# Top-k attention and two feed-forward stages on one core: the masks move to ScalarE, and the late weight matrices land elsewhere

## The chip, the cores and the metric

One core of a Trainium2 chip runs the whole program in one launch. The metric is device time in microseconds. The kernel before takes 1127.8 us, the median of three runs (1126.94 to 1128.36).

## The reference

Attention over 4 batches, 8 heads, 576 tokens of width 64, in which each query keeps its 32 largest scores; then two feed-forward blocks on 2304 tokens of width 512.

```python
scores = (q @ k.transpose(0, 1, 3, 2)) / sqrt(64)
kth = np.partition(scores, -32, axis=-1)[..., -32:-31]     # 32nd largest of each row
scores = np.where(scores >= kth, scores, -1e9)
scores = scores - scores.max(axis=-1, keepdims=True)
attn = np.exp(scores); attn = attn / (attn.sum(-1, keepdims=True) + 1e-9)
x = (attn @ v).transpose(0, 2, 1, 3).reshape(2304, 512)
h = x @ w_in                       # 512 -> 2048
x = np.maximum(0.01 * h, h) @ w_out            # 2048 -> 512
h = np.maximum(np.maximum(x @ w1, x @ w2), x @ w3)   # 512 -> 768, three times
y = h @ w_out2                     # 768 -> 512
```

The inputs are float64; the kernel takes their bit patterns as pairs of 32-bit words.

## The kernel before

**Precision.** Each float32 operand of a product is split into two float16 parts (high, and the rest, low), and three matmuls stand for one (`three`, L871). So most tiles get a ScalarE pass that writes the high part and a GpSimd subtraction that writes the low part.

**Attention.** There are 72 steps, each of two row tiles j = 0, 1 of 128 queries against 576 keys: 64 full steps (one head pair, 128 queries) and 8 steps for the last 64 queries of a batch. A step: queries times keys on PE into PSUM (L715); ScalarE copies the scores into S (L720); VectorE finds the 32nd largest value of a row in seven passes per tile, MAX8 (L735) and MATCH_REPLACE8 (L737) in turn, in the tile w; GpSimd works out a bias from the largest value (L775, L780); ScalarE writes pp = exp(scale * S + bias) with scale and bias as per-partition columns (L785). Then the mask: for j = 0 VectorE does (S >= threshold) * pp in one operation (L790); for j = 1 it writes S >= threshold as float16 over S (L794) and GpSimd multiplies pp by that (L797). ScalarE copies pp to float16 (L799), GpSimd subtracts for the low part (L801), a DMA transposes phl into pt (L804), and PE multiplies with the values (L830 to L832). There are three S, one w, one pp, one phl and one pt. Four steps finish 128 tokens of all heads (two steps for the last 64); transposes (L866) then bring them into xu, the input of a feed-forward unit.

**Feed-forward.** The 2304 tokens are ten units of 192, 128, seven times 256, and 192 tokens. A unit has a first half (`h_tile`, `y_acc`: w_in, the leaky maximum as a Prelu at L920, w_out) and a second half (`m_tile`, `o_acc`: three products, their maximum on VectorE at L1017, the last product). Unit 0's second half and all of unit 1 wait for all weights.

**Weights.** `prep_w` (L467) loads float64 words (L482), joins the words to float32 in three dependent VectorE operations per chunk of up to 512 columns (L496, L499, L502) through a PSUM tile, finds a scale, and splits into float16 parts that stay on the core. w_in has 8 parts of 1024 columns, w_out 8 of 1024, w123 18 of 512, the last matrix 8 of 384. Memory is full, so landing tiles and float32 tiles lie in zones of the weight tiles that are filled later (`ZONE`, L270). Markers such as `ZA`, `ZB`, `ZR` order the users of a zone: the landing tiles of w123 (`rw`) lie in the last matrix's region and wait for `ZB`, and the last matrix lands in the two xu buffers:

```python
"rw": [w2f[:, 2048 * i:2048 * i + 2048].bitcast(F32) for i in range(3)],   # in ZONE
...
ZT = "xu"                                                                # landing tag of the last matrix
```

**Order.** Nothing runs by itself in the order of the code. `Plan` (L72 on) collects all operations with an assumed duration, dependencies and a priority `pr`, plays them through a list schedule in which each engine takes the earliest ready operation, and of those ready within `eps` (0.03 us) the one of lowest `pr`; buffers are handed out from the counts in `NB` (L230). The resulting order is emitted, and each engine runs its part of it strictly in order. A dependent operation of the same engine is assumed to be ready 0.1 to 0.15 us after its predecessor (`LAT`). Weight operations have lower `pr` than all but the first attention steps. For w123 and the last matrix one PSUM tile (`hW`: 1) is allowed to conversion at a time.

Of the kernel before, what the change touches and what calls it, by code (L numbers as in the profile page):

```python
# [20 lines left out]
S2 = S // 2  # L21
# [185 lines left out]
def dve(n, fast=False):  # L207
    return (n / (2 if fast else 1) / 0.96 + 69) / 1000
# [11 lines left out]
def attention_moe_kernel(ctx, tc, qk, v, w_in, w_out, w123, w2o, outT):  # L220
# [31 lines left out]
    def fbuf(tag, ph, shape, dt=F32):  # L252
# [21 lines left out]
            "rw": [w2f[:, 2048 * i:2048 * i + 2048].bitcast(F32) for i in range(3)],  # L274
# [84 lines left out]
    def prep_qk(b, hp, pr, fast):  # L359
        d = dr.tile([2, 2, 2, D, S], F16, name=f"dqk{b}_{hp}")  # L360
        use_ring(("qk", b % 2, hp), 11)
        bi = col(2)
        kb = ("es", b, hp)
        for a in (1, 0):
# [19 lines left out]
        es, es2 = col(), col(2)  # L384
        op(POOL, 0.32, lambda: G.tensor_tensor(es, bi[:, 0:1], bi[:, 1:2], op=ALU.mult),
           r=[(("qk", b, hp, a), "b") for a in range(2)], w=[(kb, 0)], pr=pr)
        op(POOL, 0.32, lambda: G.tensor_scalar(es2[:, 0:1], es, 0.125, None, op0=ALU.mult),
           r=[(kb, 0)], w=[(kb, 1)], pr=pr)
        op(POOL, 0.32, lambda: G.tensor_scalar(es2[:, 1:2], es, -0.125, None, op0=ALU.mult),
           r=[(kb, 0)], w=[(kb, 2)], pr=pr)  # L390
# [69 lines left out]
    ZT = "xu"  # L460
    CVK = "iotz"
    CW = 512
    CVX = 0.0
# [3 lines left out]
    def prep_w(kind, c, parts, hi, lo, colnorm, n2c, s, bi, pr, tags, guard=((), (), []), gate=()):  # L467

        key = ("w", kind, c)
        zr = {"ra": ["ZR"], "rw": ["ZB"]}.get(tags[0], [])  # L470
        zf = {"fi": ["ZA"], "ft": ["ZA", "ZR", ("ZF", c)], "fz": ["ZB", ("ZZ", c)]}.get(tags[1], [])
        if guard[0]:
            op(POOL, 0.0, lambda: None, w=guard[0], pr=pr)
        fs, sq = [], []
        plan.eps = WEPS
        for i, saps in enumerate(parts):
            nf = sum(n for _, n in saps)
            f = buf(tags[1], [P, 768 if tags[1] in ("raw", "xu") else 512], I32)
            o = 0
            for sap, n in saps:  # L480
                raw = buf(tags[0], [P, 768])
                op(SP, 0.55, lambda raw=raw, sap=sap, n=n: Y.dma_start(raw().bitcast(I64)[:, :n], sap),  # L482
                   w=([(f, "ld")] if tags[1] in ("raw", "xu", "k2") or tags[0] in ("raw", "xu") else []) + [raw, (key, "ld")],
                   r=list(gate) + zr + (zf + [("l1", hp, a) for hp in range(HP) for a in range(2)] * (kind == "z" and ZT == "raw") + guard[2] * (tags[1] in ("raw", "xu")) if kind in "tz" else []), pr=PRW0 if (kind, c) == ("i", 0) else pr,
                   dma=dma(P * n * 8))
                for q in range(0, n, CW):
                    cw = min(CW, n - q)
                    w = lambda raw=raw, q=q, cw=cw: raw().bitcast(I32)[:, 2 * q:2 * (q + cw)].rearrange("p (n t) -> p n t", t=2)
                    t = lambda f=f, cw=cw, q=q + o: f()[:, q:q + cw]
                    pb = None  # L490
                    if kind in CVK:
                        pb = buf("acc", [P, 2, UN]) if kind in "io" else fbuf("h", "W", [P, 512])
                    m = t if pb is None else (lambda pb=pb, cw=cw, two=kind in "io": (
                        pb().rearrange("p a n -> p (a n)") if two else pb()).bitcast(I32)[:, :cw])
                    mk_ = [(f, o)] if pb is None else [pb]
                    op(DVE, dve(cw, pb is None) + CVX * (pb is not None), lambda w=w, m=m: V.tensor_scalar(  # L496
                        m(), w()[:, :, 1], 3, 0x3FFFFFFF, op0=ALU.logical_shift_left, op1=ALU.bitwise_and),
                       r=[raw] + zr + zf, w=mk_, pr=pr)
                    op(DVE, dve(cw) + CVX * (pb is not None), lambda w=w, m=m: V.scalar_tensor_tensor(  # L499
                        m(), w()[:, :, 0], 29, m(), op0=ALU.logical_shift_right, op1=ALU.bitwise_or),  # L500
                       r=[raw] + zr + zf, w=mk_, pr=pr)
                    op(DVE, dve(cw) + CVX * (pb is not None), lambda w=w, t=t, m=m: V.scalar_tensor_tensor(  # L502
                        t(), w()[:, :, 1], -0x40000000, m(), op0=ALU.bitwise_and, op1=ALU.bitwise_or),
                       r=[raw] + zr + zf + mk_ * (pb is not None), w=[(f, o)], pr=pr)
# [74 lines left out]
    def w1_prep(f, pr):  # L579
# [4 lines left out]
               (["ZA", "ZB"] if f == 0 else [], ["ZR"] if f == 0 else [("ZF", f - 2)] if f >= 3 else [],  # L584
                ["ZR"] if f < 3 else [("ZF", f - 2)]), gate=GATES[2])

    def w2_prep(e, pr):
        for hp in range(HP) if ZT == "raw" else ():
            if (1, hp) not in seen:
                seen.add((1, hp))  # L590
                prep_batch(1, hp)
        prep_w("z", e, [[(w2o[e, i], 384) for i in range(2)]], [w2[:, e, 0]], [w2[:, e, 1]],
               None, c1(cz, e), c1(sz, e), c1(bz, e), pr, (ZT, "fz" if e < 3 else ZT),
               ({0: ["ZB"], 3: [("ZZ", 2)]}.get(e, []), [("ZZ", e - 1)] if e in (1, 2) else [],
                [("ZZ", e - 1)] if e else ["ZB"]))
# [80 lines left out]
    EXPP = 4  # L676
# [3 lines left out]
    FM = 1  # L680

    def fused(i, j):
        return j < FM

    NBE = POOL
    NG, ND = (G, 0.34) if NBE == POOL else (V, 0.1)
    MODE = "N"
    NF0 = 0

    def fold(i):  # L690
        return "N" if i < NF0 else MODE

    def attention(i):
# [8 lines left out]
        Sp, wp, m = buf("S", [P, 2, S]), buf("w", [P, 2, 2, S2]), buf("m", [P, 2, TOPK + TOPK // 2 + 1])  # L702
# [19 lines left out]
        md = fold(i)  # L722
        KM = TOPK // 2
        if md == "N":
            thr = lambda j: m()[:, j, TOPK - 1:TOPK]
            tk = lambda j: [(m, j, 0, 3)]
            wj = lambda j: wp()[:, j].rearrange("p x s -> p (x s)")
            for g in range(7):
                for j in range(2):
                    r = g // 2  # L730
                    mc = lambda j=j, r=r: m()[:, j, 8 * r:8 * r + 8]
                    src = (lambda j=j: Sb[j]()) if g < 2 else (lambda j=j: wj(j))
                    rd = [(Sp, j)] if g < 2 else [(wp, j, 0)]
                    if g % 2 == 0:
                        op(DVE, dve(S) * 1.03, lambda mc=mc, src=src: V.max(mc(), src()), r=rd, w=[(m, j, 0, r)], pr=pd)  # L735
                    else:
                        op(DVE, dve(S) * 1.03 + 0.06, lambda mc=mc, src=src, j=j: V.match_replace(  # L737
                            out=wj(j), in_to_replace=mc(), in_values=src(), imm_value=NEG),
                           r=[(m, j, 0, r)] + rd, w=[(wp, j, 0)], pr=pd)
        else:  # L740
            thr = lambda j: m()[:, j, TOPK + KM:]
            tk = lambda j: [(m, j, 2)]
            for x, o in ((0, ALU.max), (1, ALU.min)):
                E, eng, du = (G, POOL, 1.32) if md == "P" else (V, DVE, 0.83)
                op(eng, du, lambda x=x, o=o, E=E: E.tensor_tensor(wp()[:, :, x], Sp()[:, :, :S2], Sp()[:, :, S2:], op=o),
                   r=[(Sp, 0), (Sp, 1)], w=[(wp, 0, x), (wp, 1, x)], pr=pd)
            for x, g in [(0, 0), (0, 1), (1, 0), (0, 2), (1, 1), (0, 3), (1, 2), (0, 4), (0, 5), (0, 6)]:
                for j in range(2):
                    r, c0 = g // 2, TOPK * x + 8 * (g // 2)
                    mc = lambda j=j, c0=c0: m()[:, j, c0:c0 + 8]  # L750
                    wx = lambda j=j, x=x: wp()[:, j, x]
                    if g % 2 == 0:
                        op(DVE, 0.375, lambda mc=mc, wx=wx: V.max(mc(), wx()), r=[(wp, j, x)], w=[(m, j, x, r)], pr=pd)
                    else:
                        op(DVE, 0.427, lambda mc=mc, wx=wx: V.match_replace(
                            out=wx(), in_to_replace=mc(), in_values=wx(), imm_value=NEG),
                           r=[(m, j, x, r)], w=[(wp, j, x)], pr=pd)
            op(DVE, 0.2, lambda: V.tensor_tensor(m()[:, :, TOPK:TOPK + KM], m()[:, :, TOPK:TOPK + KM],
                                                 m()[:, :, TOPK - 2:TOPK - 2 - KM:-1], op=ALU.min),
               r=[(m, j, 0, r) for j in range(2) for r in range(1, 4)], w=[(m, j, 1, r) for j in range(2) for r in range(2)],  # L760
               pr=pd)
            op(DVE, 0.2, lambda: V.tensor_reduce(m()[:, :, TOPK + KM], m()[:, :, TOPK - 1:TOPK + KM], axis=AX.X,
# [427 lines left out]
```

## Time and profile before

| | |
|---|---|
| median of 3 runs | 1127.8 us |
| profiled execution, first to last instruction | 1133.3 us |
| TensorE (PE) matmul busy | 918.0 us, 81% |
| VectorE (DVE) busy | 968.7 us, 85% |
| ScalarE (ACT) busy | 757.2 us, 67% |
| GpSimd (POOL) busy | 678.2 us, 60% |

The profile shows one execution; what lies around its first and last instruction isn't in it, and its span is 5.5 us above the median of the runs. Busy times are shares of the whole span; the kernel has stages with different limits, so the views by stage matter more. Matmuls overlap in the pipeline: a 256-column matmul lasts 0.27 us in the rows, and the next starts 0.11 us after it.

### The profile page before, as it was taken

What the parts mean: (1) busy time and instruction counts of PE and PEld (TensorE: products, weight loads), DVE (VectorE), ACT (ScalarE), POOL (GpSimd) and SP (SyncE); (2) the same over time, 40 slices, a digit from 0 to 9 for tenths busy, and PEclk for the clock granted to TensorE, in tenths of its full rate; (3) what the DMA queues carried; (4) which work ended last, traced back from release to release, by engine and by line L of the source; (5) the groups of instructions that cost most, each with busy time, mean ns of one, the idle gap of its engine ahead of it and who ended that gap; (6) DMA issues with size and microseconds to landing.
All of it is one profiled execution on the core that took longest, in us unless ns stands there. A gap on an engine that the chain in (4) does not pass through costs nothing.

```text
span 1133.3 us, 27397 instructions
## 1 busy us (share of the span) xinstructions
PE 918.0 (81%) x10292; PEld 803.0 (71%) x10292; DVE 968.7 (85%) x2154; ACT 757.2 (67%) x1625; POOL 678.2 (60%) x1054
## 2 busy tenths in 40 slices
PE   2253246763798998998999999889989999899998
PEld 1142235662698987887878788778878888788998
DVE  3999999899999998999898999889989998994101
ACT  7588749886578666567877766677786666555242
POOL 5476557765558565467777645666875565455221
PEclk9999997785799999999999999999999999999999
DMA  8759356766344434345673334553763443432000
GB/s 297 233 123 269 130 152 198 189 173 118 95 101 87 97 62 78 62 86 133 154 175 81 83 67 91 78 134 73 158 150 68 90 62 60 73 63 53 25 1 16
DMA packets 268517, 125.79 MB, mean 111 GB/s; under 512 B 237408, under 2 KB 255328, under 8 KB 266336
## 3 DMA queue, kind: packets, MB, share of 16 engines
q1 hardware_dynamic: 268384, 124.04, 47.1%
q8 instruction: 81, 1.33, 0.5%
q14 instruction: 52, 0.43, 0.1%
HBM read 62.65 MB, written 14.16 MB: 68 GB/s over the span
## 4 chain that ended last, share of the span: by engine, by line
PE 36%; DMA 13%; ACT 7%; POOL 5%; DVE 4%; issue 4%; SPq 1%; POOLq 0%; ACTq 0%; DVEq 0%
DMA pt<-phl 10%; PE h L872 6%; PE h L873 6%; PE h L874 6%; PE acc L872 4%; PE acc L873 4%; PE acc L874 4%; PE s L715 2%; POOL phl L801 2%; PE h L830 2%; DVE m L735 1%; DMA raw<-in_v 1%; DVE w L737 1%; PE h L831 1%; PE h L832 1%
## 5 line engine op out<-in xcount | busy, mean ns | idle before, releaser
L735 DVE MAX8 m<-w 128x8 f32<-128x576 f32 x432 | 309.1, 747 | 0.0
L933 POOL TENSOR_TENSOR f16t<-k,f16t 128x256 f16<-128x256 f32 (+2 forms) x220 | 143.0, 652 | 195.7 <-ACT f16t L927 167.9
L737 DVE MATCH_REPLACE8 w<-m,w 128x576 f32<-128x576 f32 x288 | 212.1, 742 | 0.0
L801 POOL TENSOR_TENSOR phl<-pp,phl 128x576 f16<-128x576 f32 x144 | 184.0, 1284 | 41.0 <-ACT phl L799 39.4
L872 PE MATMUL h<-k,w 128*128 128x256 f16 (+2 forms) x720 | 190.1, 268 | 8.9 <-ACT k L1013 4.6
L873 PE MATMUL h<-k,w 128*128 128x256 f16 (+2 forms) x720 | 190.1, 268 | 2.7 <-POOL k L975 2.5
L874 PE MATMUL h<-k,w 128*128 128x256 f16 (+2 forms) x720 | 189.9, 267 | 0.0
L873 PE MATMUL acc<-f16t,wo 128*128 128x256 f16 (+2 forms) x640 | 166.6, 264 | 4.4 <-POOL f16t L933 4.4
L872 PE MATMUL acc<-f16t,wo 128*128 128x256 f16 (+2 forms) x640 | 166.7, 264 | 1.2 <-ACT f16t L927 0.6
L874 PE MATMUL acc<-f16t,wo 128*128 128x256 f16 (+2 forms) x640 | 166.6, 264 | 0.0
L872 PE MATMUL h<-xu,wi 128*128 128x256 f16 (+1 forms) x576 | 154.8, 269 | 2.2 <-DVE k L502 1.3
L873 PE MATMUL h<-xu,wi 128*128 128x256 f16 (+1 forms) x576 | 154.7, 269 | 0.0
L874 PE MATMUL h<-xu,wi 128*128 128x256 f16 (+1 forms) x576 | 154.7, 269 | 0.0
L715 PE MATMUL s<-kt,qt 128*128 128x288 f16 (+5 forms) x800 | 109.1, 287 | 55.2 <-ACT S L720 48.4
L799 ACT ACTIVATE phl<-pp 128x576 f16<-128x576 f32 x144 | 97.1, 681 | 78.2 <-DMA pt<-phl 29.1
L785 ACT ACTIVATE pp<-S,nb,colt 128x576 f32<-128x576 f32 x144 | 120.9, 861 | 14.4 <-POOL nb L775 8.0
L830 PE MATMUL h<-vt,pt 128*128 128x65 f16 (+1 forms) x800 | 92.3, 203 | 45.9 <-DMA pt<-phl 37.7
L797 POOL TENSOR_TENSOR pp<-pp,S 128x576 f32<-128x576 f32 x72 | 92.1, 1279 | 56.9 <-DVE S L794 44.1
L927 ACT ACTIVATE f16t<-k 128x256 f16<-128x256 f32 (+2 forms) x220 | 86.2, 392 | 54.5 <-DVE k L1017 51.7
L920 ACT ACTIVATE k<-h,colt 128x256 f32<-128x256 f32 (+2 forms) x160 | 71.7, 452 | 73.1 <-PE h L874 71.4
L830 PEld LDWEIGHTS <-pt 128*128 128x128 f16 (+1 forms) x800 | 81.0, 106 | 54.6 <-DMA pt<-phl 52.5
L715 PEld LDWEIGHTS <-qt 128*128 128x128 f16 (+1 forms) x800 | 64.9, 109 | 75.3 <-issue 59.8
(136 smaller groups left out, 2644.8 us busy)
## 6 DMA issues: line engine op xcount, KB each, us to landing
w<-in_w SPq DMA_DIRECT2D x18, 512.0 KB, 4.4
w<-in_w_in SPq DMA_DIRECT2D x8, 1024.0 KB, 7.0
w<-in_w_out SPq DMA_DIRECT2D x8, 1024.0 KB, 4.9
raw<-in_qk SPq DMA_DIRECT2D x24, 288.0 KB, 3.4
dqk<-hl SPq DMA_DIRECT2D x48, 144.0 KB, 2.6
kt<-dqk SPq DMA_DIRECT2D x16, 288.0 KB, 3.1
qt<-dqk SPq DMA_DIRECT2D x144, 32.0 KB, 2.2
raw<-in_v SPq DMA_DIRECT2D x12, 352.0 KB, 3.7
```

The costliest lines, as they stand in the source:

```text
L715: T.matmul(p()[osl, h, o:o + w], q()[:, hh, st, :n], k()[:, hh, kc:kc + w], start=st == 0, stop=st == 1, skip_group_check=True)
L735: op(DVE, dve(S) * 1.03, lambda mc=mc, src=src: V.max(mc(), src()), r=rd, w=[(m, j, 0, r)], pr=pd)
L737: op(DVE, dve(S) * 1.03 + 0.06, lambda mc=mc, src=src, j=j: V.match_replace(out=wj(j), in_to_replace=mc(), in_values=src(), imm_value=NEG) ...
L785: op(ACT, act(S, aps=2), lambda j=j, es=es: A.activation(pp()[:, j], Sb[j](), AF.Exp, bias=nb()[:, j:j + 1], scale=es[:, 0:1]), r=[(Sp, j) ...
L797: op(POOL, pool(S), lambda j=j: G.tensor_tensor(p2(j), p2(j), mk(j), op=ALU.mult), r=[(Sp, j)], w=[(pp, j)], pr=pr)
L799: op(ACT, act(S), lambda j=j: A.activation(phl()[:, 0, j], pp()[:, j], AF.Copy), r=[(pp, j)], w=[(phl, 0, j)], pr=pr)
L801: op(POOL, pool(S), lambda j=j: G.tensor_tensor(phl()[:, 1, j], pp()[:, j], phl()[:, 0, j], op=ALU.subtract), r=[(pp, j), (phl, 0, j)], w= ...
L830: T.matmul(o, hc, vh, start=c == 0, stop=False, skip_group_check=True)
L872: T.matmul(out, wt(0), xt(0), start=first, stop=False, skip_group_check=True)
L873: T.matmul(out, wt(0), xt(1), start=False, stop=False, skip_group_check=True)
L874: T.matmul(out, wt(1), xt(0), start=False, stop=last, skip_group_check=True)
L933: op(POOL, pool(N) + 0.044, lambda: G.tensor_tensor(hl()[:, 1, :N], g()[:, 0, :N], hl()[:, 0, :N], op=ALU.subtract), r=[(g, 0), (hl, 0)], ...
```

## The change

- **Mask.** The two mask paths are gone. POOL writes nt = -threshold for both tiles, and nb = es * (threshold - max) + ln 2048 in two steps. ScalarE then writes pp = Prelu(S + nt) with slope 2^107 for negative values: what is below the threshold becomes a huge negative number, what is at or above it keeps its distance to the threshold. The Exp, now from pp to pp, turns the first into zero. The per-pair column -es is dropped, and es gets a floor of 2^-54.
- **Landing buffers.** `rw` (three tiles of 1024 float32 columns) leaves the zone and gets memory of its own, and the last matrix lands there too, not in xu; its last float32 tile is the new `fl`. The zone marker `ZB` disappears; the last matrix waits for `ZA` alone.
- **Loads.** Markers that tied a load to the earlier loads of its part and to its float32 tile are dropped.
- **Conversion.** The chunks of a part are collected as jobs; two jobs at a time go through the three stages alternately, and two PSUM tiles are allowed (`hW`: 2).
- Smaller tiles w and m; unused variants of the top-k are deleted; 1024 bytes of descriptor scratch.

```diff
-"rw": 3, "fz": 3, "rc": 2, "hH": 2, "hM": 3, "hW": 1,
+"nt": 2, ... "rw": 3, "fz": 3, "rc": 2, "fl": 1, "hH": 2, "hM": 3, "hW": 2,
-            "rw": [w2f[:, 2048 * i:2048 * i + 2048].bitcast(F32) for i in range(3)],
...
-        zr = {"ra": ["ZR"], "rw": ["ZB"]}.get(tags[0], [])
+        zr = ["ZR"] if tags[0] == "ra" else []
...
-                   w=([(f, "ld")] if tags[1] in ("raw", "xu", "k2") or tags[0] in ("raw", "xu") else []) + [raw, (key, "ld")],
-                   r=list(gate) + zr + (zf + ... + guard[2] * (tags[1] in ("raw", "xu")) if kind in "tz" else []), ...
+                   w=[raw], r=list(gate) + zr + (zf if kind in "tz" else []), ...
...
+        for x in range(0, len(jobs), 2):
+            for stage in zip(*jobs[x:x + 2]):
+                for d, fn, r, w in stage:
+                    op(DVE, d, fn, r=r, w=w, pr=pr)
...
     def w2_prep(e, pr):
-               None, c1(cz, e), c1(sz, e), c1(bz, e), pr, (ZT, "fz" if e < 3 else ZT),
+               None, c1(cz, e), c1(sz, e), c1(bz, e), pr, ("rw", "fz" if e < 3 else "fl"),
...
+        op(POOL, 0.3, lambda: G.tensor_scalar(nt(), c2(TOPK - 1), -1.0, None, op0=ALU.mult),
+           r=tk(0) + tk(1), w=[nt], pr=pr)
+        op(POOL, 0.25, lambda: G.tensor_tensor(nb(), c2(TOPK - 1), c2(0), op=ALU.subtract), ...)
         if full:
-            op(NBE, ND, lambda: NG.tensor_scalar(nb(), m()[:, :, 0:1]..., e2[:, 1:2], LNPS, op0=ALU.mult, op1=ALU.add), ...)
+            op(POOL, 0.34, lambda: G.tensor_scalar(nb(), nb(), ES[b, hps[0]], LNPS, op0=ALU.mult, op1=ALU.add), ...)
...
-            op(ACT, act(S, aps=2), lambda j=j, es=es: A.activation(pp()[:, j], Sb[j](), AF.Exp, bias=nb()[:, j:j + 1],
-                                                                  scale=es[:, 0:1]), ...)
-        for j in range(2):
-            if fused(i, j):
-                op(DVE, 0.83, lambda j=j: V.scalar_tensor_tensor(
-                    pp()[:, j], Sb[j](), thr(j), pp()[:, j], op0=ALU.is_ge, op1=ALU.mult), ...)
-            else:
-                op(DVE, 0.52, lambda j=j: V.tensor_scalar(mk(j), s2(j), thr(j), None, op0=ALU.is_ge), ...)
-                op(POOL, pool(S), lambda j=j: G.tensor_tensor(p2(j), p2(j), mk(j), op=ALU.mult), ...)
+            op(ACT, act(S, aps=1), lambda j=j: A.activation(pp()[:, j], Sb[j](), AF.Prelu, bias=nt()[:, j:j + 1],
+                                                            alpha=STEEP), r=[(Sp, j), nt], w=[(pp, j)], pr=pr)
+            op(ACT, act(S, aps=2), lambda j=j, es=es: A.activation(pp()[:, j], pp()[:, j], AF.Exp,
+                                                                   bias=nb()[:, j:j + 1], scale=es), ...)
...
-    nc = _bacc.Bacc("TRN2", target_bir_lowering=False, num_devices=1)
+    nc = _bacc.Bacc("TRN2", target_bir_lowering=False, num_devices=1, dynamic_dma_scratch_size=1024)
```

## Rows read from the trace of the kernel before

**Rows 1.** the page's slices: PE and DVE, busy tenths in 40 slices

```profile
PE   2253246763798998998999999889989999899998
...
DVE  3999999899999998999898999889989998994101
```

**Rows 2.** stages (us, busy us (count) of PE, PEld, DVE, ACT, POOL, clock, DMA, GB/s)

```profile
0.00:184.00 184.00, 67.54 (x582) 47.23 (x583) 164.60 (x356) 131.83 (x218) 107.62 (x185) 0.96 0.67 201
184.00:381.00 197.00, 149.28 (x1934) 136.95 (x1933) 187.63 (x426) 146.69 (x335) 132.25 (x213) 0.82 0.56 133
381.00:1069.00 688.00, 642.68 (x7086) 561.28 (x7085) 611.02 (x1359) 454.95 (x1011) 421.64 (x622) 0.99 0.44 90
1069.00:1134.00 65.00, 58.51 (x696) 57.53 (x694) 5.48 (x15) 23.68 (x63) 16.66 (x35) 0.98 0.05 16
...
1036.00:1064.00 28.00, 27.32 (x289) 24.11 (x289) 5.23 (x13) 9.71 (x28) 7.72 (x15) 1.00 0.12 28
1064.00:1092.00 28.00, 28.00 (x322) 27.32 (x320) 1.28 (x4) 11.06 (x29) 8.05 (x16) 1.00 0.06 20
```

**Rows 3.** groups by line and shape, DVE masks (count | busy us, mean ns | idle before)

```profile
L790 DVE SCALAR_TENSOR_TENSOR pp<-S,m,pp 128x576 f32<-128x576 f32 x72 | 60.4, 839 | 10.0 <-ACT pp L785 10.0
L794 DVE TENSOR_SCALAR S<-S,m 128x576 f16<-128x576 f32 x72 | 43.2, 600 | 1.8 <-ACT pp L785 1.8
```

**Rows 4.** the same view, ACT: attention passes, the Prelu, a scaled copy, the table load

```profile
L785 ACT ACTIVATE pp<-S,nb,colt 128x576 f32<-128x576 f32 x144 | 120.9, 861 | 14.4 <-POOL nb L775 8.0 <-POOL phl L801 6.0
L799 ACT ACTIVATE phl<-pp 128x576 f16<-128x576 f32 x144 | 97.1, 681 | 78.2 <-DMA pt<-phl 29.1 <-DVE pp L790 24.6 <-POOL pp L797 19.3
...
L920 ACT ACTIVATE k<-h,colt 128x256 f32<-128x256 f32 x112 | 53.1, 475 | 54.4 <-PE h L874 53.9
...
L352 ACT ACTIVATE raw<-raw,colt 128x576 f32<-128x576 f32 x24 | 18.4, 769 | 2.4 <-POOL colt L333 2.3
...
L341 ACT ACT_TABLE_LOAD x1 | 1.3, 1283 | 0.7 <-PEq L1182 0.7
```

**Rows 5.** the same view, POOL: mask multiply and small operations

```profile
L797 POOL TENSOR_TENSOR pp<-pp,S 128x576 f32<-128x576 f32 x72 | 92.1, 1279 | 56.9 <-DVE S L794 44.1 <-DVE colt L326 6.9 <-DVE r L837 2.1
...
L775 POOL TENSOR_SCALAR nb<-m,colt 128x2 f32<-128x2 f32 x64 | 18.1, 283 | 7.2 <-DVE m L735 1.2
...
L385 POOL TENSOR_TENSOR colt<-colt 128x1 f32<-128x1 f32 x16 | 3.5, 218 | 0.4
```

**Rows 6.** timeline, DVE (start us, us): one chunk of a conversion

```profile
176.19 0.67 DVE L496 TENSOR_SCALAR h<-w 128x512 int32<-128x512 int32 x1
176.78 0.74 DVE L735 MAX8 m<-w 128x8 f32<-128x576 f32 x1
177.44 0.67 DVE L499 SCALAR_TENSOR_TENSOR h<-w,h 128x512 int32<-128x512 int32 x1
...
178.76 0.67 DVE L502 SCALAR_TENSOR_TENSOR w<-w,h 128x512 int32<-128x512 int32 x1
```

**Rows 7.** timeline, PE and SyncE: unit starts, input transposes; issue-to-landing median

```profile
294.96 0.35 PE L872 MATMUL h<-k,w 128*128 128x192 f16 x1
...
380.40 0.27 PE L872 MATMUL h<-xu,wi 128*128 128x256 f16 x1
...
1069.81 0.24 PE L872 MATMUL h<-xu,wi 128*128 128x192 f16 x1
...
369.40 1.27 SPq L866 DMA_TRANSPOSE xu<-xhl  x1
...
1047.24 1.19 SPq L866 DMA_TRANSPOSE xu<-xhl  x1
...
xu<-xhl SPq DMA_TRANSPOSE x19, 3.0
```

**Rows 8.** PE's waits from 308 to 1036 us: total, times, longest

```profile
PE h L830 <- DMA pt<-phl: 24.6, 21, 4.6
```

**Rows 9.** the attention's transposes (tile pt): from issue to landing

```profile
DMA to landing us min/median/max: 3.9/4.8/8.0
```

More of the change, by code (lines that the diff above doesn't have):

```diff
@@ L29 @@
 LNPS = float(np.log(PS))
+STEEP = 2.0 ** 107
 P = 128
@@ L383, in prep_qk @@
                    r=[(hl, 0), (hl, 1)] + z0, w=[("d", b, hp, a, h)], pr=pr, dma=dma(P * S * 2))
-        es, es2 = col(), col(2)
+        es, es2 = col(), col()
         op(POOL, 0.32, lambda: G.tensor_tensor(es, bi[:, 0:1], bi[:, 1:2], op=ALU.mult),
            r=[(("qk", b, hp, a), "b") for a in range(2)], w=[(kb, 0)], pr=pr)
-        op(POOL, 0.32, lambda: G.tensor_scalar(es2[:, 0:1], es, 0.125, None, op0=ALU.mult),
+        op(POOL, 0.32, lambda: G.tensor_scalar(es2, es, 0.125, 2.0 ** -54, op0=ALU.mult, op1=ALU.max),
            r=[(kb, 0)], w=[(kb, 1)], pr=pr)
-        op(POOL, 0.32, lambda: G.tensor_scalar(es2[:, 1:2], es, -0.125, None, op0=ALU.mult),
-           r=[(kb, 0)], w=[(kb, 2)], pr=pr)
         ES[b, hp] = es2
@@ L489, in prep_w @@
                     t = lambda f=f, cw=cw, q=q + o: f()[:, q:q + cw]
[L490 to L504, printed above, removed]
+                    pb = buf("acc", [P, 2, UN]) if kind in "io" else fbuf("h", "W", [P, 512])
+                    m = lambda pb=pb, cw=cw, two=kind in "io": (
+                        pb().rearrange("p a n -> p (a n)") if two else pb()).bitcast(I32)[:, :cw]
+                    jobs.append((
+                        (dve(cw), lambda w=w, m=m: V.tensor_scalar(
+                            m(), w()[:, :, 1], 3, 0x3FFFFFFF, op0=ALU.logical_shift_left, op1=ALU.bitwise_and),
+                         [raw] + zr + zf, [pb]),
+                        (dve(cw), lambda w=w, m=m: V.scalar_tensor_tensor(
+                            m(), w()[:, :, 0], 29, m(), op0=ALU.logical_shift_right, op1=ALU.bitwise_or),
+                         [raw] + zr + zf, [pb]),
+                        (dve(cw), lambda w=w, t=t, m=m: V.scalar_tensor_tensor(
+                            t(), w()[:, :, 1], -0x40000000, m(), op0=ALU.bitwise_and, op1=ALU.bitwise_or),
+                         [raw, pb] + zr + zf, [(f, o)])))
                 for q in range(0, n, 512):
@@ L679, in attention_moe_kernel @@
     NCOLD = 8
[L680 to L691, printed above, removed]
     def attention(i):
@@ L721, in attention @@
                                                                p()[:, :, :288], AF.Copy), r=[p], w=[(Sp, j)], pr=pq)
[L722 to L728, printed above, removed]
-                for j in range(2):
[L730 to L735, printed above, removed]
-                    else:
[L737 to L762, printed above, removed]
-                                                 op=ALU.max),
-               r=[(m, j, 0, 3) for j in range(2)] + [(m, j, 1, r) for j in range(2) for r in range(2)],
-               w=[(m, j, 2) for j in range(2)], pr=pd)
@@ L766, in attention @@
-        p2 = lambda j: pp()[:, j].rearrange("p (a s) -> p a s", a=2)
-        s2 = lambda j: Sb[j]().rearrange("p (a s) -> p a s", a=2)
-        mk = lambda j: Sb[j]().bitcast(F16).rearrange("p (a s) -> p a s", a=2)[:, :, :S // 2]
-        nb = buf("nb", [P, 2])
+        tk = lambda j: [(m, j, 0, 3)]
+        for g in range(7):
+            for j in range(2):
+                r = g // 2
+                mc = lambda j=j, r=r: m()[:, j, 8 * r:8 * r + 8]
+                src = (lambda j=j: Sb[j]()) if g < 2 else (lambda j=j: wp()[:, j])
+                rd = [(Sp, j)] if g < 2 else [(wp, j, 0)]
+                if g % 2 == 0:
+                    op(DVE, dve(S) * 1.03, lambda mc=mc, src=src: V.max(mc(), src()), r=rd, w=[(m, j, 0, r)], pr=pd)
+                else:
+                    op(DVE, dve(S) * 1.03 + 0.06, lambda mc=mc, src=src, j=j: V.match_replace(
+                        out=wp()[:, j], in_to_replace=mc(), in_values=src(), imm_value=NEG),
+                       r=[(m, j, 0, r)] + rd, w=[(wp, j, 0)], pr=pd)
@@ L783, in attention @@
         for j in range(2):
             es = ES[b, hps[j]]
[L785 to L798 removed]
+            op(ACT, act(S, aps=1), lambda j=j: A.activation(pp()[:, j], Sb[j](), AF.Prelu, bias=nt()[:, j:j + 1],
+                                                            alpha=STEEP),
+               r=[(Sp, j), nt], w=[(pp, j)], pr=pr)
```

62 lines of the change are left out of this document (23 added, 39 removed).

## The prediction

> **What bounds the kernel now.** I read the page first, by engine and by slice [rows 1]. VectorE (DVE) is at nine tenths almost from slice 2 to slice 37, TensorE (PE) is thin up to slice 10 and at eight or nine tenths from there to the end: two engines take turns, so the kernel is read by stages. I cut it where the feed-forward units begin: unit 0 has its first matmul at 184 us, unit 2 at 381 (380.4), unit 9, the last, at 1069 [rows 7]. The view by stages [rows 2] shows four regimes. Up to 381 us DVE is busy 164.6 + 187.6 = 352.2 of 381 us, PE only 67.5 + 149.3 = 216.8: DVE sets the pace, with weight conversion and the attention's top-k. In the second of these stages PE was granted 0.82 of its clock (a mix of its two levels, 1.2 and 2.4 GHz), after a stretch in which it had been mostly idle. From 381 to 1069 PE is busy 642.7 of 688 us (93%) and DVE 611.0 (89%): both are near full, and each waits a little for the other. After 1069 only PE matters.
>
> The transposes that complete a unit's input show which of the two is late [rows 7]: the one that completes unit 2's is issued at 369.4, 11 us before that unit's first matmul (380.4); the last one at 1047.2, 22 us before unit 9's. So PE is already the later of the two at both ends of the long stage, and a faster attention by itself moves the end only by what PE idles. Between the two transposes lie 54 attention steps, 677.8 / 54 = 12.55 us each.
>
> **The change, part by part.** Masks: DVE loses 72 fused multiplies and 72 comparisons, 60.4 + 43.2 = 103.6 us, 1.44 per step [rows 3]. Its 14 top-k passes per step stay. GpSimd (POOL) loses 92.1 us of mask multiplies and gains 72 small two-column operations for the negated threshold, like the one of 283 ns, and 72 subtractions, like the one of 218 ns: 20.4 + 15.7 = 36 us [rows 5]; it ends 56 us lighter. ScalarE (ACT) gains 144 Prelus of 576 columns with one pointer operand. None of that shape is in the trace. Below is the plain copy of 681 ns, above the Exp with two pointers, 861 ns; the copy scaled by one pointer, 769 ns, is the nearest row [rows 4], so 144 x 0.769 = 111 us (98 to 124). The Exp keeps its two pointers and its price.
>
> One rule of the skill speaks against such a move. In this trace the DVE mask takes 839 ns fused, or 600 ns with 1279 ns of POOL behind it, and the ACT pass 769 ns [rows 3 to 5]: the move trades equal times. The Trainium skill (ScalarE: Activation LUTs, Rules for kernel authors) sends relu and max to VectorE, up to about three times faster in bf16. By that, 144 masks would be 144 x 0.769 / 3 = 37 us on DVE, an estimate from the page's factor, and the move would win a third of what I count; the float32 rows disagree, and they decide.
>
> The masks on the path: until unit 2 starts, 18 steps are done, and DVE, the pace there, loses 18 x 1.44 = 26 us. Unit 2's input can then be complete at 369.4 - 26 + 3 = 347 (3.0 us for its landing [rows 7]).
>
> Conversion in pairs: of the third matrix's 18 chunks and the fourth's 8, each passes three dependent DVE operations, and today an attention operation slips between any two: stages start at 176.19, 177.44 and 178.76 with a MAX8 in the first gap, so a chunk takes some 3.2 us for 1.8 us of work [rows 6]. In pairs the gaps are filled by the other chunk. DVE's work stays the same; the last weights come up to 26 x 1.3 = 34 us sooner, and attention that ran in the gaps comes later. Own landing buffers and unordered loads: the third matrix no longer waits until the first two have left the region it lands in, the fourth no longer lands in the two buffers of the units' inputs. Below, this is worth nothing; above, it adds to the 34 us of the pairs and the 19 us that DVE saves on the 13 masks before then, and the second half of unit 0 comes from 295 [rows 7] to 250 or less. That work isn't the path by itself, but units 0 and 1 must be off PE before unit 2: unit 0's second half to unit 2's start takes 381 - 295 = 86 us now, and some 5 us more with more attention steps among it. From 250 it would be over at 341, before the input is there (347). From 295 - 19 = 276 (masks alone) it would end at 367. I take 350, since the landing of weights is paced by three buffers and by ACT's passes too; ends 347 and 367.
>
> Other edits (one spare column per head pair, smaller top-k tile, less scratch memory for descriptors) cost nothing that a row shows: they remove one 227-ns operation per pair and otherwise only hold space, and the DMA issues here are SyncE's own.
>
> From unit 2 on: PE's work stays 642.7 us to unit 9's start and 64.3 to the end. DVE falls from 611.0 to 611.0 - 54 x 1.44 = 533 and can't hold PE any more; ACT rises from 455.0 to 455.0 + 54 x 2 x 0.769 = 538, 10.0 us per step, and the step's chain has the Prelu, the Exp and the copy in one queue behind the top-k, where now the Exp runs ahead of it. So PE's idle time decides. Upper end: the 45.3 us of now (688 - 642.7), more than half of whose named waits are for the transposes that feed the attention's second product, 24.6 us [rows 8], which the change doesn't touch. Lower end: when attention is over, PE idles 0.7 of 56 us, 1.2%, or 8 us of 650 [rows 2]. I take 25, the middle, since neither end's cause is gone.
>
> Sum: 350 + 642.7 + 25 + 64.3 = 1082 us of span, against 1133.3. The span of the profiled execution is 5.5 us above the median of the runs (1127.8), and the profile shows no time around it; I take the 5.5 off: 1076.5. Ends: 347 + 642.7 + 8 + 64.3 = 1062, or 1056.5; 367 + 642.7 + 45.3 + 64.3 = 1119, or 1114.
>
> **Rivals.** *ScalarE passes the gain on:* with 10.0 us of work per step of about 12, the evictions of the feed-forward wait behind Prelu, Exp and copy (2.3 us for each half of a step), the matmuls behind them wait too, and PE idles as before: 350 + 642.7 + 45.3 + 64.3 - 5.5 = 1097. For it: PE's evictions are ACT's and come in program order. Against it: ACT is at 66% in that stage now, and its idle time before the copies is mostly waiting for others [rows 4].
>
> *Slower, by one blocked queue:* there is one pp, one phl and one pt. A step's copies may not write phl before the transposes of the step before have landed, 4.8 us median and 8.0 at most after issue [rows 9], and ACT, in order, stands still at the copy with every eviction behind it. A step then costs ACT's 10.0 us plus that stand. With attention as the bound the span is 350 + 54c + 70 (landing and unit 9), which is 1133 at c = 13.2 us. So it decides from 3.2 us of stand per step on; at 4.0 it is 350 + 756 + 70 - 5.5 = 1170. Against it: ACT's idle time before all its copies is 78.2 us, 1.1 per step, of which 29.1 for the transposes [rows 4], and Prelu and Exp of the next step fill the wait as long as pp is free.
>
> *Slower, by table switches:* Prelu and Exp alternate in each step now. If they needed different tables, two loads per step of the 1283 ns that the one load takes [rows 4] would bring ACT from 538 to 538 + 54 x 2 x 1.283 = 677 us in the long stage; with the waits that its copies have now (78.2 us for 144, so 59 for 108) that stage is 736 us, and the sum 350 + 736 + 64.3 - 5.5 = 1145, the 18 steps before it left out. Against it: Prelu stands among the Exps already (112 times in the unit evictions alone) and the trace has one load [rows 4]. The Trainium skill (ScalarE: Activation LUTs, Table sets: the hidden batching unit) asks for calls to be grouped by set for that reason; by the trace these two are in one.
>
> *No gain:* the masks went from an engine that wasn't late. If the weights came no sooner than the masks allow and PE idled 60 us after 381, it is 367 + 643 + 60 + 64 - 5.5 = 1128.
>
> **How the numbers follow.** Forecast (PE bound, some idle, 1056 to 1092): 0.58. ScalarE passes it on, or the start gains little (1092 to 1114): 0.24. Better than 1056, if PE's clock and idle improve together: 0.07. Within 0.2%, which is what a measurement of this kernel can tell (2.3 us): 0.04. Slower: 0.05 for the blocked queue, 0.02 for the tables. Range 1055 to 1112; faster 0.89, same 0.04, slower 0.07.
>
> **What would show it.** Right: one table load; Prelu near 0.77 us; DVE without the two mask lines and below 85% from unit 2 on; no attention operation between the stages of a paired chunk; unit 0's second half from 250 to 275 and unit 2 at about 350; PE at 95 to 97% from there to the end. Wrong: PE's waits on ACT's evictions in the tens of us (ScalarE passes it on); ACT's wait at the copy above 3 us per step; attention steps still 12.5 us apart with PE below 93%.

## The result, and the profile after

The changed kernel takes 1083.2 us (median of 4 runs, 1079.3 to 1086.7) against 1128.1 us for the kernel before: ratio 0.959, 95% interval 0.957 to 0.962, a gain of 45 us. The forecast was 1076.5 us with a range of 1055 to 1112: the sign was right, and the time lies within the range, 6.7 us above the figure.

The profiled execution took 1083.9 us with a span of 1081.9; the sum of the prediction, before its offset, was a span of 1082. First the page's slices, PE, DVE and the clock granted to PE:

```profile
PE   2334334498998998998999899999989999999998
...
DVE  3999999998999999999649899989599999910101
...
PEclk9995556689999999999999999999999999999999
```

DVE now has holes (the 6, 4 and 5 from slice 20 on) and PE beside them has none: the long stage belongs to PE. Next the view by stages, cut near the first matmuls of units 0, 2 and 9 (which come at 196.8, 352.3 and 1020.2), then the long stage once more, from first matmul to first matmul (columns as in [rows 2]):

```profile
0.00:193.00 193.00, 72.59 (x614) 50.51 (x615) 173.76 (x377) 151.53 (x254) 110.15 (x199) 0.73 0.70 217
193.00:350.50 157.50, 132.72 (x1864) 125.54 (x1864) 149.06 (x358) 141.19 (x328) 102.35 (x206) 0.90 0.56 127
350.50:1022.00 671.50, 641.84 (x7173) 565.24 (x7174) 548.27 (x1264) 526.56 (x1132) 373.27 (x677) 1.00 0.41 94
1022.00:1082.00 60.00, 54.12 (x646) 53.14 (x643) 5.17 (x13) 21.63 (x58) 14.25 (x29) 0.99 0.05 17
...
352.30:1020.20 667.90, 638.96 (x7140) 562.78 (x7141) 546.47 (x1260) 524.64 (x1128) 371.01 (x675) 1.00 0.41 94
```

Against [rows 2], everything before unit 2 shrank by some 30 us, with DVE still its busiest engine (322.8 of 350.5 us). In the long stage PE's work is the same 642 us, its idle time 30 us instead of 45; DVE fell from 89% to 82%, ScalarE rose from 66% to 78%. The unit starts, from PE's timeline (start us, us), and the two input transposes, from SyncE's:

```profile
259.77 0.25 PE L811 MATMUL h<-k,w 128*128 128x192 f16 x1
...
352.32 0.28 PE L811 MATMUL h<-xu,wi 128*128 128x256 f16 x1 [0.51 <-DMA xu<-xhl]
...
1020.24 0.25 PE L811 MATMUL h<-xu,wi 128*128 128x192 f16 x1
```
```profile
349.40 1.23 SPq L805 DMA_TRANSPOSE xu<-xhl  x1
...
973.76 1.20 SPq L805 DMA_TRANSPOSE xu<-xhl  x1
```

At unit 2 PE waits for its input now (2.9 us from transpose to first matmul, where it was 11 [rows 7]); at unit 9 the transpose is issued 46 us ahead of the first matmul, where it was 22. Between lie 54 attention steps of 11.56 us (12.55 before). The masks, by line and shape, ACT and then POOL:

```profile
L735 ACT ACTIVATE pp<-pp,nb,colt 128x576 f32<-128x576 f32 x144 | 123.1, 862 | 0.2
L732 ACT ACTIVATE pp<-S,nt 128x576 f32<-128x576 f32 x144 | 107.8, 768 | 13.0 <-POOL phl L740 8.6 <-POOL nt L718 3.8
L738 ACT ACTIVATE phl<-pp 128x576 f16<-128x576 f32 x144 | 96.6, 680 | 5.1 <-DMA pt<-phl 4.6
...
L340 ACT ACT_TABLE_LOAD x1 | 1.3, 1283 | 0.7 <-PEq L1121 0.7
```
```profile
L718 POOL TENSOR_SCALAR nt<-m 128x2 f32<-128x2 f32 x72 | 15.7, 218 | 30.9 <-DVE m L708 27.4 <-DVE colt L325 1.6 <-DVE r L776 0.8
L720 POOL TENSOR_TENSOR nb<-m 128x2 f32<-128x2 f32 x72 | 14.1, 195 | 0.1
```

Prelu takes 768 ns (forecast 769), there is one table load, and the copy that idled 78.2 us [rows 4] idles 5.1. PE's waits in the long stage (total us, times, longest):

```profile
PE s L693 <- ACT S L698: 6.2, 6, 2.8
PE h L769 <- DMA pt<-phl: 4.6, 7, 1.1
PE h L812 <- POOL k L914: 3.4, 6, 1.4
```

The wait for the attention's transposes, 24.6 us in [rows 8], is down to 4.6; the prediction had it stay.

### The profile page after: what moved, and what is told of

It reads as the page before. It is cut to its first block, busy times and chain, and to the rows that moved or that the text cites. A ratio compares the mean times of both kernels' runs of the same rounds, so it can differ in the third digit from the quotient of the medians.

```text
span 1081.9 us, 27366 instructions
## 1 busy us (share of the span) xinstructions
PE 901.3 (83%) x10292; PEld 794.4 (73%) x10292; DVE 876.3 (81%) x2010; ACT 840.9 (78%) x1769; POOL 600.0 (55%) x1110
## 4 chain that ended last, share of the span: by engine, by line
PE 49%; DVE 19%; DMA 11%; ACT 10%; POOL 5%; issue 4%; SPq 2%; POOLq 0%; ACTq 0%; DVEq 0%
PE h L811 8%; PE h L812 8%; PE h L813 8%; DMA pt<-phl 6%; DVE m L708 5%; PE acc L811 5%; PE acc L812 5%; PE acc L813 5%; DVE w L710 5%; PE s L693 4%; DVE acc L487 2%; PE h L769 2%; POOL phl L740 2%; DVE w L493 2%; PE h L770 2%
## 5 line engine op out<-in xcount | busy, mean ns | idle before, releaser
L872 POOL TENSOR_TENSOR f16t<-k,f16t 128x256 f16<-128x256 f32 (+2 forms) x220 | 136.7, 623 | 190.0 <-ACT f16t L866 165.6
L811 PE MATMUL h<-k,w 128*128 128x256 f16 (+2 forms) x720 | 187.2, 264 | 9.4 <-ACT k L912 4.8
L812 PE MATMUL h<-k,w 128*128 128x256 f16 (+2 forms) x720 | 187.2, 264 | 4.4 <-POOL k L914 4.1
L813 PE MATMUL h<-k,w 128*128 128x256 f16 (+2 forms) x720 | 187.4, 265 | 0.0
L735 ACT ACTIVATE pp<-pp,nb,colt 128x576 f32<-128x576 f32 x144 | 123.1, 862 | 0.2
L708 DVE MAX8 m<-S 128x8 f32<-128x576 f32 x144 | 103.1, 744 | 19.5 <-ACT S L698 19.3
L732 ACT ACTIVATE pp<-S,nt 128x576 f32<-128x576 f32 x144 | 107.8, 768 | 13.0 <-POOL phl L740 8.6
L812 PEld LDWEIGHTS <-w 128*128 128x128 f16 x960 | 94.3, 98 | 19.6 <-issue 11.0
L698 ACT ACTIVATE S<-s 128x576 f32<-128x576 f32 x144 | 92.6, 643 | 18.6 <-PE s L693 17.7
```

The lines of the kernel that those rows point to most:

```text
L698: op(ACT, act(S, True), lambda t=t, p=p: A.activation(t().rearrange("p (a s) -> p a s", a=2), p()[:, :, :288], AF.Copy), r=[p], w=[(Sp, j) ...
L732: op(ACT, act(S, aps=1), lambda j=j: A.activation(pp()[:, j], Sb[j](), AF.Prelu, bias=nt()[:, j:j + 1], alpha=STEEP), r=[(Sp, j), nt], w=[ ...
L735: op(ACT, act(S, aps=2), lambda j=j, es=es: A.activation(pp()[:, j], pp()[:, j], AF.Exp, bias=nb()[:, j:j + 1], scale=es), r=[(nb, j), ((" ...
L811: T.matmul(out, wt(0), xt(0), start=first, stop=False, skip_group_check=True)
L812: T.matmul(out, wt(0), xt(1), start=False, stop=False, skip_group_check=True)
L813: T.matmul(out, wt(1), xt(0), start=False, stop=last, skip_group_check=True)
```

## The experiments

Each ratio is to runs of the kernel before on the same chip, with its 95% interval. Those runs had medians of 1128.1 to 1131.8 us, so kernels of different groups are compared by ratio, or by median with some 4 us of doubt.

### Which part of the change pays

**The masks alone**, in the kernel before, with the smaller tiles w and m, everything else as it was:

```diff
 (before.py)  - fused mask L790, comparison L794, POOL multiply L797
              + nt = -threshold; pp = Prelu(S + nt); pp = Exp(pp), as in the change
```

> The kernel before with only the Prelu masks; landing buffers, load order and unpaired conversion stay as they were. Theory (first stage paced by VectorE, then TensorE the bound): VectorE loses 26 us on the 18 steps before unit 2, but the weights come late, so unit 0's second half starts at about 276 and unit 2 at 362 to 367; from there 642 us of TensorE work, 30 idle, 60 for unit 9: about 1100 us. Rival A (the masks are all of the gain): 1083. Rival B (the masks were on an engine that wasn't late, and the gain came from the weights): 1115 to 1128.

1091.1 us, 0.964 (0.961 to 0.966). That lies between its theory (1100) and its rival A (1083). The new masks by themselves give 41 us against the runs of before beside them (1131.8), 37 against 1128.1: most of the 45. Its stages:

```profile
0.00:366.00 366.00, 214.49 (x2596) 182.43 (x2597) 343.89 (x782) 309.37 (x609) 223.13 (x421) 0.79 0.63 174
366.00:1027.50 661.50, 636.58 (x7036) 560.49 (x7035) 528.10 (x1216) 511.01 (x1103) 361.60 (x659) 0.99 0.43 92
```

Unit 0's second half starts at 281.8 and unit 2 at 366.0; the prediction worked out 276 and 367 for "masks alone". In the profiled executions, from first matmul to first matmul, the part before unit 2 is 14 us shorter than in the kernel before (366.0 against 380.4), the long stage 28 us (661.5 against 689.4) and the rest 2 us: two thirds of what the masks give come from the long stage. PE waits 4.8 us for the attention's transposes here too, so it is the masks that took that wait away.

**The rest alone**: the changed kernel with the old masks.

```diff
 (after.py)   - nt, Prelu, Exp from pp
              + the old fused mask for j = 0, comparison and POOL multiply for j = 1
```

> The changed kernel with the old masks (VectorE multiply for one tile, VectorE comparison and GpSimd multiply for the other). Theory: attention is as slow as before (12.5 us per step), unit 2's input comes at about 370, at most 10 us are won before it, and the long stage is as before: 1115 to 1125 us. Rival A (masks are all): 1128. Rival B (the weights are the gain): 1085 to 1100.

1145.2 us, 1.011 (1.007 to 1.014): slower than before by 1%, outside all three forecasts, which would make the two parts far from additive. Its weights do come early (unit 0's second half at 270.4, before 295.0), yet the long stage takes 698.5 us, with 650 us of PE work (643 before). With another order of the schedule (the tie window of the list schedule at 0.04 instead of 0.03) it is the same:

> Landing buffers and pairs with the old masks, tie window 0.04. Theory A (the 12 us by which it lost to the kernel before are the order's chance): 1120 to 1140, away from 1145. Theory B (something in the loads costs the long stage): 1143 to 1148 again.

1143.8 us, 1.011 (1.009 to 1.014). In both, SyncE spends longer on a transpose of the attention (at least 2441 and 2438 ns) than in any of the twelve other kernels (at least 1743 to 1776). The reason was looked for in the memory map of the compiled programs: without the small tile nt, all tiles behind it begin 64 bytes lower, and phl and pt stand 192 bytes past a multiple of 256 instead of on one, as they do in all the other kernels. So the last run put an unused nt back:

```diff
 (loads_only) + "nt": 2 buffers; at the first step POOL writes one of them once (2 columns)
```

> loads_only (after's loads and pairs with the old masks, 1145.2 us) plus one unused two-column tile nt, written once at the first step, so that all attention tiles behind it (nb, pp, phl, pt) move up by that tile and stand as far apart from m as in after. Nothing is left out. In loads_only the attention's transposes (phl to pt) take the SyncE queue at least 2441 ns each to issue (median 2831), in every other kernel at least 1746 (median about 2000 to 2139). Theory 'place of the tiles': the issue falls back to about 1.75 us at least, 2.0 median, VectorE's and PE's waits fall with it, and the time comes to 1128 to 1135. Rival 'order of the schedule': the issue stays at 2.4 to 2.8 us and the time at 1140 to 1147. Third: the issue falls but the time stays at 1140 or more; then the slow issue was not what made loads_only slow.

1121.4 us, 0.992 (0.988 to 0.995): 24 us faster (21 by the ratios) for a tile that nobody reads, below even the range of the first theory. Without the tile, the transposes of tile pt (issue, ns min/median/max; and from issue to landing), then the stages:

```profile
L762 SPq DMA_TRANSPOSE pt<-phl x72: 2441/2831/4358, 49.0 to 1053.6; - x72
...
DMA to landing us min/median/max: 4.5/4.9/7.3
```
```profile
0.00:381.50 381.50, 207.68 (x2483) 177.42 (x2484) 347.93 (x771) 276.12 (x549) 236.33 (x394) 0.92 0.61 164
381.50:1080.00 698.50, 649.67 (x7127) 564.01 (x7128) 619.26 (x1369) 458.94 (x1016) 427.30 (x626) 0.99 0.45 89
```

With it, the same two views:

```profile
L765 SPq DMA_TRANSPOSE pt<-phl x72: 1776/2106/4077, 49.3 to 1031.7; - x72
...
DMA to landing us min/median/max: 3.9/4.3/7.7
```
```profile
0.00:379.20 379.20, 208.39 (x2482) 179.09 (x2483) 346.76 (x770) 276.34 (x548) 236.21 (x395) 0.91 0.60 165
379.20:1058.00 678.80, 644.55 (x7126) 563.78 (x7127) 619.13 (x1370) 459.37 (x1016) 429.32 (x626) 0.99 0.42 92
```

The fastest issue falls by 0.67 us, PE's wait for these transposes in the long stage from 23.2 to 11.7 us, and 20 us come off the long stage (5 of them PE's busy time). The added operation moves the order of the schedule too, so not all of the 24 us is proved to come from the place; but two orders at the bad place gave 1145 and 1144, and both had the slow issue, while no order with the tiles on a multiple of 256 has it. The parts now agree with the whole: the masks alone 0.964, the rest alone 0.992, and 0.964 x 0.992 = 0.956, where the whole change has 0.959.

**The pairs**, taken out of the changed kernel:

```diff
-for x in range(0, len(jobs), 2): for stage in zip(*jobs[x:x + 2]):     ("hW": 2)
+for x in range(0, len(jobs), 1): for stage in zip(*jobs[x:x + 1]):     ("hW": 1)
```

> The changed kernel with one conversion job at a time and one PSUM tile for it; masks and landing buffers as changed. Theory: attention operations slip between a chunk's stages again, the last weights come some 20 us later, unit 0's second half at 270 and unit 2 at 360 in place of 352: 1088 to 1095 us. Rival (the landing buffers alone bring the weights early): 1083 as with pairs.

1077.9 us, 0.952 (0.950 to 0.954), 5 us faster than the changed kernel (8 by the ratios) and the fastest version run. Unit 0's second half starts at 258.8, with pairs at 259.8. That isn't because the pairs do nothing. The DVE timeline of the changed kernel shows the two chunks taking turns in places, and a top-k pass between two stages in others (start us, us):

```profile
172.23 0.67 DVE L490 SCALAR_TENSOR_TENSOR h<-rw,h 128x512 int32<-128x512 int32 x1
...
172.95 0.73 DVE L710 MATCH_REPLACE8 w<-m,S 128x576 f32<-128x576 f32 x1
173.61 0.67 DVE L493 SCALAR_TENSOR_TENSOR w<-rw,h 128x512 int32<-128x512 int32 x1
...
176.76 0.69 DVE L487 TENSOR_SCALAR h<-rw 128x512 int32<-128x512 int32 x1
177.35 0.68 DVE L493 SCALAR_TENSOR_TENSOR w<-rw,h 128x512 int32<-128x512 int32 x1
177.95 0.69 DVE L490 SCALAR_TENSOR_TENSOR h<-rw,h 128x512 int32<-128x512 int32 x1
```

Over the 26 chunks of the two late matrices, 23 top-k passes stand between the stages of a chunk with pairs and 35 without, and the last weights are ready sooner. GpSimd writes the low part of the last one here, in the changed kernel and then without pairs (before: at 295.47):

```profile
230.19 1.66 POOL L353 TENSOR_TENSOR w<-fl,w 128x768 f16<-128x768 f32 x1
```
```profile
246.89 1.65 POOL L353 TENSOR_TENSOR w<-fl,w 128x768 f16<-128x768 f32 x1 [0.52 <-ACT w L352]
```

So the pairs bring the last weight 17 us sooner, but unit 0's second half no longer waits for it. On PE it follows directly on the last matmul of the unit's own first half (without pairs that one comes at 252.66):

```profile
259.69 0.25 PE L813 MATMUL acc<-f16t,wo 128*128 128x192 f16 x1
259.77 0.25 PE L811 MATMUL h<-k,w 128*128 128x192 f16 x1
```

### Which engine paces which stage

**More work for VectorE**, one unused pass per step, in the 54 late steps or the 18 early ones (planned at 0.84 us, 45 and 15 us in all; the rows show 1.01 and 0.94 us, 54.5 and 16.9 us); **more for ScalarE**, every Prelu of the late steps twice (83 us):

```diff
+if i >= 18:    (dve_early: i < 18)
+    V.scalar_tensor_tensor(w[:, 0], S, threshold, w[:, 0], op0=is_ge, op1=mult)
```
```diff
 A.activation(pp, S, Prelu, bias=nt, alpha=STEEP)
+if i >= 18: A.activation(pp, S, Prelu, bias=nt, alpha=STEEP)
```

> The changed kernel with one more VectorE pass (like the old fused mask, 0.84 us, its result unused) in each of the 54 steps from step 18 on: 45 us of work on VectorE behind unit 2's start. Theory (TensorE is the bound there, VectorE has 123 of 671 us to spare): within 4 us of the changed kernel's 1083. Rival (VectorE is still the pace of the long stage): 1083 + 45 = 1128, and half of that if both engines take turns.

> The same pass in each of the 18 steps before unit 2: 15 us of VectorE work in the first stage. Theory (VectorE paces that stage): unit 2 starts 15 us later, 1095 to 1098 us. Rival (the weights, not VectorE, pace it): 1083.

> The changed kernel with each Prelu run twice (same result) in the 54 steps from step 18 on: 83 us more ScalarE work, 527 + 83 = 610 of 671 us. Theory (TensorE is the bound, ScalarE's spare time takes some of it): up to 15 us more, 1085 to 1098. Rival (ScalarE has become the bound of the long stage): 1083 + 60 to 83 = 1143 to 1166.

1085.7 us (0.960, 0.957 to 0.964), 1096.1 (0.970, 0.967 to 0.972) and 1091.9 (0.966, 0.964 to 0.968). The long stage of the first and PE's wait for the attention's transposes in it, then the same of the third:

```profile
349.90:1024.30 674.40, 643.36 (x7158) 565.67 (x7157) 596.37 (x1319) 524.39 (x1132) 397.87 (x676) 0.99 0.42 93
...
PE h L773 <- DMA pt<-phl: 7.8, 10, 1.4
```
```profile
351.70:1025.70 674.00, 642.07 (x7121) 564.54 (x7121) 552.11 (x1258) 588.05 (x1230) 370.96 (x671) 0.99 0.43 94
...
PE h L773 <- DMA pt<-phl: 8.6, 10, 2.3
```

Against 671.5 us in the changed kernel the stage is 3 us longer, though DVE is busy 48 us more, or ScalarE 61: neither paces it. (The whole kernel takes 3 and 9 us more, which the order alone can do, as the next runs show.) DVE is back at 88% there, as in the kernel before (89%), and the long wait for the transposes does not come back: VectorE's load by itself does not make it. The 17 us in the early steps cost 13 (11 by the ratios), and unit 2 starts at 362.2 instead of 352.3. That fits a first stage paced by DVE, as its 92% busy time does, but a reordering alone can do nearly as much.

### What the order alone is worth

The same operations under the wider tie window, for the changed kernel and for the one without pairs:

> The changed kernel with the schedule's tie window EPS at 0.04 in place of 0.03 us: the same operations in a slightly different order. It measures what the order alone is worth. If order is worth 1 us, 1082 to 1085 us; if it is worth as much as the 5 us between paired and unpaired conversion, 1075 to 1092.

> Unpaired conversion with the tie window at 0.04. Theory A (pairs are worth nothing, and the 5 us are the order's chance): anywhere in 1075 to 1092, no nearer to 1078 than the paired kernel of the same window. Theory B (pairs cost 5 us): 5 us below the paired kernel of the same window.

1092.1 us (0.967, 0.965 to 0.968) and 1090.2 (0.963, 0.961 to 0.966): 9 and 12 us slower, with no operation added or taken away. In the first, 7 us are lost before unit 2 (359.2); in the second, 6 before it and 9 in the long stage. (The third such pair, the changed kernel with the old masks, differs by 1 us.) So a difference below some 12 us between two single versions can't be laid to an edit: not the 5 to 8 us of the pairs, not the 8 to 10 of the loads, and the 11 to 13 of the early passes only with doubt. The some 40 us of the masks and the 21 to 24 of the tile's place are beyond it.

### Two attempts to go further

**Two more small units**, 128 columns wide in place of one of 256, to start unit 2 earlier:

```diff
+UNITS = [192, 128, 128, 128] + [256] * 6 + [192]
```

> Unpaired conversion, and the first 256-token unit split in two of 128 tokens, so that unit 2's input is there after 14 steps, not 18. Theory (TensorE idles 8 us between 252 and 350 and unit 2 needn't wait for step 18): 3 to 8 us less, 1070 to 1075. Rival (more and shorter ScalarE and GpSimd passes eat it, or TensorE has no free time there): 1076 to 1085.

1085.1 us, 0.960 (0.957 to 0.963). Unit 2 starts at 347.2 (350.6 without this), but PE has 9 us more work in the long stage (647.3 us in 7815 matmuls, 638.4 in 7141 without this). The 7 us by which the kernel is slower are again within what the order can do.

**The first conversion stage into the float tile in SBUF** instead of PSUM, so that no PSUM tile is held:

```diff
-m() = (w[:, :, 1] << 3) & 0x3FFFFFFF          # m: PSUM
-m() = (w[:, :, 0] >> 29) | m()
+t() = (w[:, :, 1] << 3) & 0x3FFFFFFF          # t: the float tile, SBUF
+m() = (w[:, :, 0] >> 29) | t()
```

> The changed kernel, but the first conversion stage writes the float32 tile in SBUF, not a PSUM tile. If that runs in half the time (0.35 us for 0.69), VectorE loses 58 x 0.3 = 17 us before unit 2, and as VectorE is the pace there the time falls by 10 to 17 us, to about 1070. If the stage takes as long as into PSUM, nothing changes: 1083. If the pace of the first stage isn't VectorE: 1083 with a shorter stage.

1105.6 us, 0.976 (0.973 to 0.978), 22 us slower than the changed kernel (18 by the ratios). The second stage now reads two operands from SBUF. Changed kernel, then this one:

```profile
L490 DVE SCALAR_TENSOR_TENSOR acc<-w,acc 128x512 int32<-128x512 int32 x32 | 21.0, 696 | 0.0
...
L490 DVE SCALAR_TENSOR_TENSOR h<-rw,h 128x512 int32<-128x512 int32 x18 | 12.3, 689 | 0.0
```
```profile
L487 DVE TENSOR_SCALAR w<-w 128x512 int32<-128x512 int32 x32 | 22.7, 723 | 0.9 <-DMA w<-in_w_in 0.9
...
L490 DVE SCALAR_TENSOR_TENSOR acc<-w 128x512 int32<-128x512 int32 x18 | 16.4, 951 | 0.0
L490 DVE SCALAR_TENSOR_TENSOR acc<-w,w 128x512 int32<-128x512 int32 x14 | 11.7, 867 | 0.0
...
L487 DVE TENSOR_SCALAR w<-rw 128x512 int32<-128x512 int32 x9 | 7.7, 861 | 0.0
...
L490 DVE SCALAR_TENSOR_TENSOR h<-rw,k 128x512 int32<-128x512 int32 x9 | 7.2, 804 | 0.0
...
L487 DVE TENSOR_SCALAR k<-rw 128x512 int32<-128x512 int32 x9 | 4.4, 487 | 0.7 <-DMA rw<-in_w 0.7
```

The second stage's 0.69 us became 0.80 to 0.95, and the first stage (L487), hoped for at 0.35, took 0.72 or 0.86 in 41 of the 50 full chunks and 0.49 in nine. VectorE is busy 14 us more in all, and unit 2 starts at 372.8, 20 us later; the assumed duration of the first stage was halved too, so the order differs, and part of the loss can be the order's. The Trainium skill (SBUF — State Buffer, Who interferes with whom) says that a VectorE instruction with two SBUF inputs contends with a GpSimd instruction that reads SBUF; the longer rows agree, though no run here separates GpSimd's part.

## Why the prediction was right

*The start of unit 2* (forecast 350, measured 352.3). That DVE paces this part fits the runs, and the mechanism held: DVE lost the mask work, and unit 0's second half had to come early enough to be out of the way. It came at 259.8, within the 250 to 275 named. The run with the masks alone confirms the bound without early weights: the last transpose for unit 2's input is issued at 339.7 there, yet the unit starts only at 366.0 (worked out: 367; in it, unit 0's second half came 6 us later than worked out and took 7 us less, so the close hit is partly luck).

Three terms were off:

- The pairs got "up to 26 x 1.3 = 34 us sooner" and brought the last weight 17 us sooner. The sign "no attention operation between the stages of a paired chunk" did not come true.
- The sum had no term for unit 0's own first half, which ends at 259.7 and is now what the second half waits for; so the 17 us of the pairs bring nothing here.
- The reason given for 350 was the landing of weights, but the last wait before unit 2 is for its input (PE is free 0.51 us sooner). It is issued at 349.4, where 343 was worked out: the attention that the early weights displaced, which the prediction named and did not price, or the order's chance.

The landing buffers and freer loads, counted as nothing from below, bring most of the weights' gain (the last one is written from 295.5 us on before, 281.0 with the masks alone, 246.9 without pairs, 230.2 in the changed kernel). The last matrix is loaded from 193.7 us on, before from 229.4. SyncE's issues of its 8 loads, before and after (ns min/median/max, first and last start):

```profile
L482 SPq DMA_DIRECT2D xu<-in_w2o x8: 328/376/526, 229.4 to 283.6; - x8
```
```profile
L476 SPq DMA_DIRECT2D rw<-in_w2o x8: 327/334/456, 193.7 to 214.1; - x8
```

*The long stage* (forecast 642.7 of work + 25 idle = 667.7; measured 667.9 between the unit starts, 639.0 of work and 28.9 idle). The size is right by a choice of the middle, which is luck; the reasoning for the upper end failed. The wait for the attention's transposes "which the change doesn't touch" fell from 24.6 to 4.6 us. Before, the copy into phl waited for DVE's and POOL's masks and for the last transposes (78.2 us, [rows 4]); now 5.1 us. That the step's tail got shorter and its transposes so came in time is the reading of these rows; the run with the masks alone shows that the masks do it, not by which of these waits. More load on VectorE does not bring the wait back (88% busy in the run with late passes, wait 7.8 us), and a longer tail by itself hardly does (every Prelu twice, wait 8.6 us). The GpSimd multiply, which went with the old masks (92.1 us, [rows 5]), was not tried by itself.

*Engine loads.* DVE fell by 92.4 us (forecast 103.6), ScalarE rose by 83.7 (forecast 111), though the Prelu's mean is as forecast. The term that was mis-sized is count times mean: consecutive passes overlap. On the ACT timeline two Prelus in a row last 1.44 us, not 1.54, an overlap of 0.10 between two neighbours:

```profile
610.16 1.44 ACT L732 ACTIVATE pp<-S,nt 128x576 f32<-128x576 f32 x2 [1.20 <-POOL phl L740]
```

An added pass of 0.77 us made ScalarE busier by 83.7 / 144 = 0.58 us, and the 108 doubled ones of the experiment by 61 / 108 = 0.57, about the mean less one overlap at each end. GpSimd fell by 78 us (forecast 56); the new small operations cost 30 of the 36 us counted, and where the other 16 come from was not looked into. None of this decided here, since neither VectorE nor ScalarE paces the long stage.

*The tail* (forecast 64.3, measured 61.7). *The offset*: the one term of the sum that cost something. The 5.5 us by which the profiled execution of before lay above the median were taken off the sum; but the span of the changed kernel's profiled execution, 1081.9, lies below its runs' median of 1083.2, and each run is some 2 us above its own span (1083.9 and 1081.9, 1079.3 and 1077.3). The gap of before was that one execution's, not a constant of the kernel; without it the forecast would have been 1082 to 1084.

*The rivals.* Table switches: one load. A queue blocked at the copy: 5.1 us in all, where 3.2 per step would have decided. ScalarE passes the gain on: 108 more Prelus lengthen the long stage by 3 us. No gain: the masks alone take 14 us off the part before unit 2 and 28 off the long stage.

## What to carry to other kernels

Price a move between engines by stage: here a nearly equal trade of pass times won some 40 us, a third of it before unit 2, where VectorE is the busiest engine, and two thirds in the long stage, where PE hardly waits any more for the end of the attention's chain. Count what a pass adds to an engine by its mean less the overlap with its neighbours on the timeline. When an input is made to come sooner, look for what its user waits for next: here the second half of unit 0 ran into its own first half. Before laying a few us to an edit in a statically ordered kernel, run the same operations in another order, and look whether a tile that came or went has shifted the places of the others.

## What the runs showed of the hardware

What a DMA transpose costs went with the place of its tiles: with phl and pt 192 bytes past a multiple of 256 its issue takes at least 2441 ns on SyncE, on a multiple 1776, and landing 4.5 instead of 3.9 us at best. The units' transposes (xhl to xu, issue at least 1193 and 1195 ns) did not change, though xhl had moved in the same way; xu had moved too, from 64 bytes past a multiple onto one. Whether phl or pt is the one that matters was not tried. The Trainium skill (DMA: Bandwidth & Descriptors, How a descriptor splits into AXI transactions) says that a descriptor that doesn't start on a 256-byte boundary is fetched from the boundary below and costs extra beats; the direction agrees, and no run here shows whether that is the cause.

The same integer shift from SBUF to SBUF took 487 ns in one pair of tiles and 861 in another (L487 in the last experiment). What sets the two apart was not tried.
